# LSH attention and MLP on one core: one product for two heads' value means, value tiles summed on GpSimd, a new instruction order

## The chip, the core and the metric

The kernel runs on one core of a Trainium2 chip. The core has TensorE (PE) for matrix products, VectorE (DVE), ScalarE (ACT) and GpSimd (POOL) for elementwise work, and SyncE (SP), which issues DMAs. Each engine runs its own instructions in the order in which the program has them, and waits at semaphores for the others. The metric is the device time of one execution in microseconds.

## The reference, cut to what matters

```python
# q, k, v: (4, 8, 768, 64); proj: (64, 6); x: 3072 rows of 512
mask   = bucket(q) == bucket(k)                  # 6 sign bits of q@proj and k@proj
scores = where(mask, 0.125 * q @ k.T, -1e9)
attn   = exp(scores - max(scores)); attn = attn / (sum(attn) + 1e-9)
x      = (attn @ v), the heads side by side
h      = maximum(x @ w_in, 0)
out    = (s * h*h + b) @ w_out
```

The kernel adds to each row of `attn @ v` a small multiple of the sum of the head's value rows, `1e-9 / (768 + 1e-9)` times it, so that a row without any match comes out as the mean of the values, as the reference has it. This vector, one of 64 numbers for each head (`vmn`), is what the change is about.

## The kernel before, in words

There are 32 heads (4 batches of 8), called visits and counted from 0, and each is worked in three chunks of 256 queries, so 96 slots. A slot's work is a chain: score products on TensorE into three PSUM banks (L595 for the fp32 heads, L597 for the others), the row maximum on VectorE (L603), two small transposes on TensorE (L614, L618) with short VectorE steps behind them (L616, L625), six mask products that add the maximum into the banks (L635, L637), exponentials on ScalarE (L642), and value products into bank 3 (L665 for the first nine heads, L667 and L668 for the rest). Two copies on ScalarE (L698, L700) read bank 3 and so free it for the next slot; L700 adds `vmn`. Each pair of heads is scaled on GpSimd (L710), cast on ScalarE (L711), split on GpSimd (L712) and written to DRAM by a DMA from the tile `xsb`.

From slot 23 on TensorE also has the products of the MLP (L746, L763), which fill its time between the attention's steps. In the first slots ScalarE, VectorE and GpSimd also decode the MLP's weights (L374 to L386), which is why GpSimd is busy there.

How the mean's sum is made depends on the head. Heads 0 to 8 are computed in fp32 (`w < NPL`, NPL is 9): their value tile `EV`, 128 rows by 6 tiles by 64, is multiplied on TensorE by a column of ones, one product for each of the 6 tiles into one column of bank 4 (L543). Heads 9 to 31 load the tile into `vn`, VectorE sums it over the 6 tiles into 64 columns of `pj` (L556), and one product with the ones follows (L558). In both cases ScalarE scales the column into `vmn` (L525). An fp32 product shows as two records in the trace, so L543 has 108 for 9 heads and L558 has 46 for 23. Bank 4 is shared with the transposes: a group of steps holds it until it is done.

The order on all engines is not the order of the code. Each step is added to a plan with an engine, a cost, what it reads and writes, and a priority (`pr`); a list scheduler goes through the plan with these costs and takes the step of lowest priority that is ready. The priority is the slot's number times 10 and an offset, and to it a number of the table NUDGE is added, one for each place of the code and part of the program. So a change of the table or of a cost moves steps on all engines.

Of the kernel before, what the change touches and what calls it, by code (L numbers as in the profile page):

```python
# [22 lines left out]
EPS = 1e-9  # L23
# [143 lines left out]
NPL = 9  # L167
# [5 lines left out]
def lsh_attention_moe(ctx: ExitStack, tc, q, k, v, proj, w_in, w_out, s, b, out):  # L173
# [52 lines left out]
    def mmc(n, c):  # L226
        return c * (n / 2400.0 + 0.0013) if c % 4 == 0 else c * (n * 0.000436 + 0.0088)
# [124 lines left out]
    def decode(u, pr):  # L352
# [9 lines left out]
        def raw():  # L362
            return box["t"]
# [12 lines left out]
        dve(256, lambda: nc.vector.tensor_scalar(raw()[:, :, 1], gi, -2**31, None, ALU.bitwise_and), [gk], rk, pr, 0.6)  # L376
        dve(512, lambda: nc.vector.scalar_tensor_tensor(gi, gi, 3, raw()[:, :, 1], ALU.logical_shift_left, ALU.bitwise_or), rk, [gk], pr, 0.92)
# [8 lines left out]
        pool(512, lambda: nc.gpsimd.tensor_tensor(wt[key][:, 1], g, f32(wt[key][:, 0]), ALU.subtract), [gk, key + (0,)], [key + (1,)], pr)  # L386
# [135 lines left out]
    def mean(bb, h, pr):  # L522

        n = bb % 2 * H + h
        act(1, lambda: nc.scalar.activation(vmn[:, n:n + 1], bank[0:D, 4, 0:1], AF.Copy, scale=EPS / (S + EPS)), [("b", 4, "m")], [("vm", n)], pr)  # L525
        plan.hold(None)

    def prep_values(w, pr):
# [4 lines left out]
        if w < NPL:  # L533
# [6 lines left out]

            def sums():
                for t in range(NT):
                    nc.tensor.matmul(bank[0:D, 4, 0:1], EV[x][:, t, 0], ones, start=(t == 0), stop=(t == NT - 1))  # L543
            plan.hold(4)
            pe(0.5, sums, vk, [("b", 4, "m")], pr)
            mean(bb, h, pr)
            return
# [4 lines left out]
        to = vn  # L552
        plan.add(SP, 0.7, lambda: nc.sync.dma_start(to, vd), [], ["vn"], pr, 0.9)
        act(NT * D, lambda: nc.scalar.copy(VS[x][:, :, 0, :], to), ["vn"], vk[0:1], pr)
        pool(NT * D, lambda: nc.gpsimd.tensor_tensor(VS[x][:, :, 1, :], to, f32(VS[x][:, :, 0, :]), ALU.subtract), ["vn", vk[0]], vk[1:2], pr)
        dve(NT * D, lambda: nc.vector.tensor_reduce(pj[:, 0:D], to.rearrange("p t d -> p d t"), AX.X, ALU.add), ["vn"], ["vp"], pr, 0.84)  # L556
        plan.hold(4)
        pe(0.25, lambda: nc.tensor.matmul(bank[0:D, 4, 0:1], pj[:, 0:D], ones, start=True, stop=True), ["vp"], [("b", 4, "m")], pr)  # L558
        mean(bb, h, pr)
# [397 lines left out]
```

## Time and profile before

| what | value |
|---|---|
| median of 3 timed runs | 1003.89 us (1003.73 to 1006.42) |
| profiled execution | 1000.88 us, its span 999.1 us |
| TensorE busy | 979.9 us (98%) |
| VectorE busy | 677.5 us (68%) |
| ScalarE busy | 670.8 us (67%) |
| GpSimd busy | 640.5 us (64%) |
| mean share of the 16 DMA engines | q1 29.9%, q10 5.7% |

Busy time is that of one profiled execution. Products on TensorE overlap in the records, so the time that one takes is read from start to start. In the chain of work that ended last, TensorE has 91%, VectorE, GpSimd and DMA 2% each.

### The profile page before, as it was taken

How to read it: one execution, taken by the hardware profiler on the slowest of the kernel's cores; microseconds unless marked ns; L12 is line 12 of the kernel's file. 1: busy time of each engine (PE TensorE's matmuls, PEld its weight loads, DVE VectorE, ACT ScalarE, POOL GpSimd, SP SyncE). 2: the span in 40 equal slices, each digit the busy share in tenths (PEclk: the TensorE clock that was granted, in tenths of full speed). 3: DMA queues.
4: the chain of work that ended last, by engine and by line, in shares of the span. 5: the costliest groups of instructions: out<-in, count | busy, mean ns of one | idle time of the engine just before them, and what ended most of it. 6: DMA issues, size and time to landing. Idle time of an engine off the chain costs nothing.

```text
span 999.1 us, 18150 instructions
## 1 busy us (share of the span) xinstructions
PE 979.9 (98%) x6528; PEld 883.6 (88%) x6528; DVE 677.5 (68%) x1030; ACT 670.8 (67%) x1312; POOL 640.5 (64%) x584
## 2 busy tenths in 40 slices
PE   8989989999999999999999999999999999999998
PEld 6877868889999999999999999999999999999997
DVE  6777888778778877878778877878778766200000
ACT  4677777767767777777767777777777777523232
POOL 1677776758677677768677677778677677522222
PEclk9999999999999999999999999999999999999999
DMA  7575664533423423433423432433423310201000
GB/s 195 148 192 162 182 169 129 152 76 82 129 53 79 122 69 63 131 71 81 120 63 79 104 84 61 136 71 81 120 60 80 97 47 1 96 1 64 32 22 21
DMA packets 131954, 93.06 MB, mean 93 GB/s; under 512 B 101145, under 2 KB 104601, under 8 KB 131865
## 3 DMA queue, kind: packets, MB, share of 16 engines
q1 hardware_dynamic: 126664, 74.87, 29.9%
q10 hardware_dynamic: 5200, 17.05, 5.7%
q8 instruction: 51, 0.84, 0.3%
q14 instruction: 39, 0.31, 0.1%
HBM read 48.24 MB, written 18.87 MB: 67 GB/s over the span
## 4 chain that ended last, share of the span: by engine, by line
PE 91%; DVE 2%; POOL 2%; DMA 2%; issue 1%; ACT 1%; DVEq 0%; ACTq 0%; SPq 0%; POOLq 0%
PE bank L746 28%; PE bank L763 27%; PE bank L597 6%; PE bank L637 6%; PE bank L667 5%; PE bank L668 5%; PE bank L665 4%; PE bank L595 2%; PE bank L695 2%; DMA xd<-xsb 1%; PE bank L618 1%; PE bank L506 1%; PE bank L508 1%; PE bank L507 1%; POOL w L386 1%
## 5 line engine op out<-in xcount | busy, mean ns | idle before, releaser
L661 POOL TENSOR_TENSOR hl<-et,hl 128x512 fp32r<-128x512 f32 x207 | 267.3, 1320 | 138.5 <-ACT hl L660 86.0
L746 PE MATMUL bank<-xc,w 128*128 128x256 f32 x2304 | 338.5, 284 | 0.0
L746 PEld LDWEIGHTS bank<-xc,w 128*128 128x128 f32 x2304 | 305.4, 190 | 5.9
L763 PE MATMUL bank<-w,ghb 128*128 128x512 f32 x768 | 252.4, 396 | 0.0
L754 POOL TENSOR_TENSOR glb<-rb,ghb 128x512 fp32r<-128x512 f32 x96 | 124.1, 1292 | 99.8 <-ACT ghb L753 93.7
L603 DVE TENSOR_REDUCE mx<-bank 128x256 f32<-128x1536 f32 x96 | 168.0, 1750 | 6.9 <-PE bank L597 3.2
L763 PE MATMUL bank<-w,glb 128*128 128x512 f32 x384 | 152.3, 398 | 0.0
L642 ACT ACTIVATE et<-bank 128x512 f32<-128x512 f32 x234 | 128.6, 626 | 32.5 <-PE bank L637 23.4
L763 PEld LDWEIGHTS bank<-w,ghb 128*128 128x128 f32 x768 | 135.2, 189 | 16.6 <-issue 0.2
L687 DVE TENSOR_REDUCE zb<-et 128x256 f32<-128x1536 f32 x69 | 120.8, 1751 | 40.9 <-ACT et L642 40.2
L660 ACT CAST hl<-et 128x512 fp32r<-128x512 f32 x207 | 125.2, 672 | 0.3
L751 ACT ACTIVATE rb<-bank 128x512 f32<-128x512 f32 x96 | 56.8, 592 | 98.7 <-PE bank L746 98.4
L597 PE MATMUL bank<-aq,ks 84*128 84x256 f32 x504 | 109.6, 301 | 2.3 <-DMA aq<-nat 1.4
L700 ACT ACTIVATE xpb<-bank,vmn 64x256 f32<-64x256 f32 x96 | 45.0, 468 | 97.4 <-PE bank L668 64.1
L667 PE MATMUL bank<-hl,vs 128*128 128x256 f32 x414 | 107.9, 283 | 0.0
L668 PE MATMUL bank<-hl,vs 128*128 128x256 f32 x414 | 107.3, 281 | 0.0
L597 PEld LDWEIGHTS bank<-aq,ks 84*128 84x128 f32 x504 | 81.0, 190 | 9.1 <-ACT xpb L700 1.8
L667 PEld LDWEIGHTS bank<-hl,vs 128*128 128x128 f32 x414 | 77.9, 188 | 8.9
L668 PEld LDWEIGHTS bank<-hl,vs 128*128 128x128 f32 x414 | 78.0, 188 | 8.0
L763 PEld LDWEIGHTS bank<-w,glb 128*128 128x128 f32 x384 | 72.2, 188 | 11.5 <-issue 0.2
L637 PE MATMUL bank<-bq,ks 128*128 128x256 f32 x504 | 76.9, 287 | 0.0
L771 DVE SCALAR_TENSOR_TENSOR osb<-bank,misc,bcs 128x512 f32<-128x512 f32 x22 | 16.2, 747 | 88.9 <-PE bank L763 88.8
(126 smaller groups left out, 1545.2 us busy)
## 6 DMA issues: line engine op xcount, KB each, us to landing
xd<-xsb SPq DMA_DIRECT2D x48, 256.0 KB
xc<-xd SPq DMA_DIRECT2D x48, 256.0 KB
raw<-in_moe_w_in_dram ACTq DMA_DIRECT2D x16, 512.0 KB
raw<-in_moe_w_out_dram ACTq DMA_DIRECT2D x16, 512.0 KB
out_dram<-osb SPq DMA_DIRECT2D x22, 256.0 KB
ks<-aq SPq DMA_DIRECT2D x28, 192.0 KB
ks<-bq SPq DMA_DIRECT2D x28, 192.0 KB
bq<-aq SPq DMA_DIRECT2D x28, 192.0 KB
```

Of the source, the lines that this page charges most:

```text
L597: nc.tensor.matmul(o, ks[0:HR + NR, 0, kt], aq[0:HR + NR, cs], start=m == 0, stop=m == 1, skip_group_check=True)
L603: dve(S * TPC, lambda: nc.vector.tensor_reduce(t, sc, AX.XY, ALU.max), [("b", b) for b in pb], [tk], pr, 1.75)
L637: nc.tensor.matmul(o, ks[:, 1, kt], bq[:, cs], start=False, stop=m == 1, skip_group_check=True)
L642: act(512, lambda p=p, z=z: nc.scalar.activation(et(z) if plain(i) else pairs(z), bank[:, pb[p]] if plain(i) else bank[:, pb[p]].rearrange ...
L660: act(512, lambda z=z, y=y: nc.scalar.copy(HL[2 * y].rearrange("p (m n) -> p m n", n=CH), pairs(z)), [("e", z)], [("hl", 2 * y)], pr, 0.05)
L661: pool(512, lambda z=z, y=y: nc.gpsimd.tensor_tensor(HL[2 * y + 1].rearrange("p (m n) -> p m n", n=CH), pairs(z), f32(HL[2 * y]).rearrange ...
L667: nc.tensor.matmul(av, VS[x][:, kt], HL[2 * y][:, ms], start=(kt == 0), stop=False)
L668: nc.tensor.matmul(av, VS[x][:, kt], HL[2 * y + 1][:, ms], start=False, stop=(kt == NT - 1))
L687: dve(S * TPC, lambda: nc.vector.tensor_reduce(ZB, es, AX.XY, ALU.add), [("e", z) for z in range(NE)], ["zb"], pr, 1.75)
L746: nc.tensor.matmul(hp, wt[("wi", n, cc)][:, m % 2, fs], xc[:, m // 2, :], start=(cc == 0 and m == 0), stop=(cc == NC_ - 1 and m == 2))
L754: pool(2 * CH, lambda r=r, gh=gh, gl=gl: nc.gpsimd.tensor_tensor(gl, r, f32(gh), ALU.subtract), [rk, hk], [lk], MP)
L763: nc.tensor.matmul(bank[:, 6 + t, :], (gh, gh, gl)[n][:, ts], wt[("wo", f)][:, n % 2], start=(f == 0 and n == 0), stop=(f == NF - 1 and n ...
```

## The change

It has three parts.

1. Heads 9 to 31: an even head `h` sums its own value tile and that of head `h + 1`, which is loaded into `vn` a second time for that, into 2 x 64 columns of `pj`. One product with 128 columns of weights makes both sums, and the two evictions to `vmn` read rows 0 to 63 and 64 to 127 of the column. Odd heads after head 9 make none. That is 12 products (11 of them for two heads) in place of 23, and 34 loads of `vn` in place of 23. VectorE's sums stay 23.
2. Heads 2 to 8: GpSimd adds the six value tiles, in three additions of 192, 64 and 64 columns into `vn`, and one product follows in place of six. Heads 0 and 1 keep the six.
3. A few costs of the plan are other numbers, and the table NUDGE is new, so that steps stand in another order on every engine. Line numbers from L538 on move: L595/L597 become L621/L623, L618 is L644, L637 is L663, L642 is L668, L665 is L691, L698/L700 are L724/L726, L711 is L737, L746 is L772, L763 is L789.

```diff
-        return c * (n / 2400.0 + 0.0013) if c % 4 == 0 else c * (n * 0.000436 + 0.0088)
+        return c * (n / 2400.0 + 0.0013) if c % 4 == 0 else c * {256: 0.1215, 384: 0.175, 512: 0.2345}[n]
...
-    def mean(bb, h, pr):
+    def mean(bb, h, pr, j=0):
...
-        act(1, lambda: nc.scalar.activation(vmn[:, n:n + 1], bank[0:D, 4, 0:1], AF.Copy, scale=EPS / (S + EPS)), [("b", 4, "m")], [("vm", n)], pr)
-        plan.hold(None)
+        act(1, lambda: nc.scalar.activation(vmn[:, n:n + 1], bank[j * D:(j + 1) * D, 4, 0:1], AF.Copy, scale=EPS / (S + EPS)), [("b", 4, "m")], [("vm", n)], pr)
...
+            if w > 1:
+                s1, s2 = vn[:, 0:3], vn[:, 3]
+                pool(3 * D, lambda: nc.gpsimd.tensor_tensor(s1, EV[x][:, 0:3, 0], EV[x][:, 3:6, 0], ALU.add), vk[0:1], ["vn"], pr, 0.56)
+                pool(D, lambda: nc.gpsimd.tensor_tensor(s2, vn[:, 0], vn[:, 1], ALU.add), [], ["vn"], pr, 0.27)
+                pool(D, lambda: nc.gpsimd.tensor_tensor(s2, vn[:, 3], vn[:, 2], ALU.add), [], ["vn"], pr, 0.27)
+                plan.hold(4)
+                pe(0.3, lambda: nc.tensor.matmul(bank[0:D, 4, 0:1], s2, ones, start=True, stop=True), ["vn"], [("b", 4, "m")], pr)
+                mean(bb, h, pr)
+                plan.hold(None)
+                return
...
-            pe(0.5, sums, vk, [("b", 4, "m")], pr)
+            pe(0.75, sums, vk, [("b", 4, "m")], pr)
...
-        dve(NT * D, lambda: nc.vector.tensor_reduce(pj[:, 0:D], to.rearrange("p t d -> p d t"), AX.X, ALU.add), ["vn"], ["vp"], pr, 0.84)
+        def sums(j, to, tk):
+            dve(NT * D, lambda: nc.vector.tensor_reduce(pj[:, j * D:(j + 1) * D], to.rearrange("p t d -> p d t"), AX.X, ALU.add), [tk], ["vp"], pr, 0.84)
...
+        if h % 2 and w > NPL:
+            return
+        heads = (h,) if h % 2 else (h, h + 1)
+        for j, h_ in enumerate(heads):
+            if j:
+                fetch(to, tk, v[bb, h_].rearrange("(p t) d -> p t d", t=NT))
+            sums(j, to, tk)
+        rows = len(heads) * D
         plan.hold(4)
-        pe(0.25, lambda: nc.tensor.matmul(bank[0:D, 4, 0:1], pj[:, 0:D], ones, start=True, stop=True), ["vp"], [("b", 4, "m")], pr)
-        mean(bb, h, pr)
+        pe(0.3, lambda: nc.tensor.matmul(bank[0:rows, 4, 0:1], pj[:, 0:rows], ones, start=True, stop=True), ["vp"], [("b", 4, "m")], pr)
+        for j, h_ in enumerate(heads):
+            mean(bb, h_, pr, j)
...
 NUDGE = {
-    0: {0: -25.2, 1: 58.1, 2: 23.3, 3: 60, 4: -47.5},
+    0: {0: 28.7, 1: -23.1, 2: -11.6, 3: 14.5, 4: -8.9},
```

What the built order shows at three places, before and then after. First TensorE at the mean of head 4 (its value tile is `eva`, the second use of that tile), in the slot whose mask products read `bq_71`. Before:

```order
L665 MATMUL bank<-ex_87,vs_208 128x256 x2
L618 MATMUL bank<-ident,nmt 8x128
L543 MATMUL bank<-misc,eva 64x1 x6
L637 MATMUL bank<-bq_71,ks_73 128x256 x6
L472 MATMUL bank<-ident,nat_67 128x128 x3
```

After:

```order
L691 MATMUL bank<-ex_87,vs_208 128x256 x2
L623 MATMUL bank<-aq_69,ks_73 128x256 x2
L644 MATMUL bank<-ident,nmt 8x128
L623 MATMUL bank<-aq_69,ks_73 128x256 x2
L546 MATMUL bank<-misc,vn 64x1
L663 MATMUL bank<-bq_71,ks_73 128x256 x6
```

One product from `vn` stands where six from `eva` stood, still between the second transpose and the mask products, and two score products now stand between the transpose and it.

Second ScalarE, at the second cast of `xsb` (L711, now L737), with the copies that free bank 3. Before:

```order
L380 CAST w_644<-osb 128x512
L642 ACTIVATE et<-bank 128x512 x2
L711 CAST xsb<-xpb 128x256
L698 ACTIVATE zpb<-bank 64x256
L700 ACTIVATE xpb<-bank,vmn 64x256
L642 ACTIVATE et<-bank 128x512
```

After:

```order
L726 ACTIVATE xpb<-bank,vmn 64x256
L724 ACTIVATE zpb<-bank 64x256
L461 ACTIVATE eqa<-bank,misc 128x384
L737 CAST xsb<-xpb 128x256
L374 ACTIVATE osb<-raw_218 128x512
```

The two copies stood behind the cast and now stand ahead of it.

Third TensorE, in the second chunk of head 2 (its value tile is `vs_208`): the mask products and the value products of the same slot. Before:

```order
L637 MATMUL bank<-bq_70,ks_72 128x256 x6
L665 MATMUL bank<-et,vs_208 128x256 x2
L597 MATMUL bank<-aq_69,ks_73 128x256 x4
L665 MATMUL bank<-ex_82,vs_208 128x256
L614 MATMUL bank<-ident,mx 128x128 x2
```

After:

```order
L663 MATMUL bank<-bq_70,ks_72 128x256 x6
L691 MATMUL bank<-ex_82,vs_208 128x256 x2
L623 MATMUL bank<-aq_69,ks_73 128x256 x2
L691 MATMUL bank<-ex_83,vs_208 128x256 x2
L640 MATMUL bank<-ident,mx 128x128 x2
```

Two value products of the slot before (from `et`) and four score products stood between the mask products and the first value product of their slot (from `ex_82`); now it stands directly behind them.

## Rows read from the trace of the kernel before

**Rows 1.** Stretches of the span: us, busy time of each engine, clock, DMA share, GB/s.
```profile
5.00:155.00 150.00, 136.26 (x800) 111.61 (x800) 115.42 (x174) 106.65 (x211) 95.40 (x80) 0.99 0.66 176
155.00:805.00 650.00, 649.30 (x4477) 594.69 (x4476) 519.78 (x778) 478.97 (x953) 469.38 (x431) 1.00 0.37 92
```

**Rows 2.** Waits of TensorE from 5 to 155 us: total us, times, longest.
```profile
PE bank L665 <- ACT xpb L700: 3.9, 4, 2.1
PE bank L597 <- DMA aq<-nat: 1.4, 1, 1.4
...
PE bank L614 <- DVE mx L603: 0.3, 1, 0.3
```

**Rows 3.** Order of time on TensorE near 785 us: start us, us, operation, count.
```profile
784.20 0.28 PE L668 MATMUL bank<-hl,vs 128*128 128x256 f32 x1
784.32 0.40 PE L763 MATMUL bank<-w,ghb 128*128 128x512 f32 x1
784.55 0.88 PE L637 MATMUL bank<-bq,ks 128*128 128x256 f32 x6
785.36 0.28 PE L558 MATMUL bank<-misc,pj 128*64 128x1 f32 x2
785.57 0.50 PE L763 MATMUL bank<-w,ghb 128*128 128x512 f32 x1
```

**Rows 4.** Weight loads by line: busy us, mean ns, idle time before them.
```profile
L665 PEld LDWEIGHTS bank<-ex,vs 128*128 128x128 f32 x120 | 20.7, 190 | 4.4 <-ACT xpb L700 1.8
...
L614 PEld LDWEIGHTS bank<-ident,mx 128*128 128x128 f32 x48 | 6.3, 141 | 3.5 <-DVE mx L603 1.2 <-DVE bq L481 0.4 <-ACT eqb L461 0.2
...
L558 PEld LDWEIGHTS bank<-misc,pj 128*64 128x64 f32 x46 | 4.4, 134 | 3.3 <-issue 0.4
```

**Rows 5.** DMA issues of vn, then SyncE's waits before them.
```profile
vn<-in_v_dram SPq DMA_DIRECT2D x23, 192.0 KB
...
SPq L553 <- POOL vs L555: 6.8, 11, 1.1
```

**Rows 6.** Order of time on TensorE near 152 us.
```profile
151.21 0.86 PE L543 MATMUL bank<-misc,evb 128*64 128x1 f32 x12
152.00 0.98 PE L637 MATMUL bank<-bq,ks 128*128 128x256 f32 x6
152.91 0.86 PE L543 MATMUL bank<-misc,vs 128*64 128x1 f32 x12
```

**Rows 7.** GpSimd by line: busy us, mean ns, idle time before them.
```profile
L386 POOL TENSOR_TENSOR w<-osb,w 128x512 fp32r<-128x512 f32 x32 | 45.6, 1429 | 12.4 <-ACT w L380 11.0 <-DMA raw<-in_moe_w_out_dram 0.7 <-DMA nat<-in_k_dram 0.7
L378 POOL TENSOR_TENSOR osb<-osb,raw 128x512 int32<-128x512 int32 x32 | 41.9, 1308 | 47.4 <-DVE osb L377 35.1 <-ACT raw L375 6.1 <-issue 2.1
...
L710 POOL TENSOR_TENSOR xpb<-xpb,zpb 128x256 f32<-128x256 f32 x48 | 36.4, 758 | 41.0 <-DVE zpb L709 15.8 <-DVE xpb L702 13.0 <-ACT et L642 9.1
L555 POOL TENSOR_TENSOR vs<-vn,vs 128x384 fp32r<-128x384 f32 x23 | 23.3, 1014 | 4.9 <-ACT vs L554 4.9
```

**Rows 8.** Order of time on ScalarE near 65 us.
```profile
64.85 0.40 ACT L711 CAST xsb<-xpb 128x256 fp32r<-128x256 f32 x1 [1.99 <-DMA xd<-xsb]
...
65.68 0.47 ACT L700 ACTIVATE xpb<-bank,vmn 64x256 f32<-64x256 f32 x1
```

**Rows 9.** Order of time on TensorE near 66 us.
```profile
66.29 1.93 PE L665 MATMUL bank<-et,vs 128*128 128x256 f32 x4 [2.06 <-ACT xpb L700]
68.02 0.42 PE L618 MATMUL bank<-ident,nmt 128*8 128x128 f32 x1
```

**Rows 10.** One stretch after the wait; the clock stands behind GpSimd.
```profile
66.30:69.60 3.30, 3.30 (x10) 2.54 (x11) 1.17 (x5) 2.09 (x4) 1.23 (x2) 0.52 0.98 280
```

**Rows 11.** Order of time near 152 us, the exponentials.
```profile
152.54 1.08 ACT L642 ACTIVATE ex<-bank 128x512 f32<-128x512 f32 x2 [0.27 <-PE bank L637]
```

**Rows 12.** The decode step L376: min/median/max ns; then busy us, mean ns.
```profile
L376 DVE TENSOR_SCALAR raw<-osb x32: 373/478/1848, 21.5 to 202.4; 128x512 int32<-128x512 int32 x32
...
L376 DVE TENSOR_SCALAR raw<-osb 128x512 int32<-128x512 int32 x32 | 23.1, 720 | 0.2
```

More of the change, by code (lines that the diff above doesn't have):

```diff
@@ L375, in decode @@
         act(512, lambda: nc.scalar.activation(raw()[:, :, 0], raw()[:, :, 0].bitcast(U32), AF.Copy, scale=float(2.0**-29)), rk, rk, pr, 0.06)
-        dve(256, lambda: nc.vector.tensor_scalar(raw()[:, :, 1], gi, -2**31, None, ALU.bitwise_and), [gk], rk, pr, 0.6)
-        dve(512, lambda: nc.vector.scalar_tensor_tensor(gi, gi, 3, raw()[:, :, 1], ALU.logical_shift_left, ALU.bitwise_or), rk, [gk], pr, 0.92)
+        dve(256, lambda: nc.vector.tensor_scalar(raw()[:, :, 1], gi, -2**31, None, ALU.bitwise_and), [gk], rk, pr, 0.72)
+        dve(512, lambda: nc.vector.scalar_tensor_tensor(gi, gi, 3, raw()[:, :, 1], ALU.logical_shift_left, ALU.bitwise_or), rk, [gk], pr, 0.8)
         pool(512, lambda: nc.gpsimd.tensor_tensor(gi, gi, raw()[:, :, 0], ALU.add), rk, [gk], pr)
@@ L385, in decode @@
                 pool(512, lambda: nc.gpsimd.tensor_tensor(bcs, bcs, g, ALU.add), [gk], ["bcs"], pr + 5)
-        pool(512, lambda: nc.gpsimd.tensor_tensor(wt[key][:, 1], g, f32(wt[key][:, 0]), ALU.subtract), [gk, key + (0,)], [key + (1,)], pr)
+        pool(512, lambda: nc.gpsimd.tensor_tensor(wt[key][:, 1], g, f32(wt[key][:, 0]), ALU.subtract), [gk, key + (0,)], [key + (1,)], pr, 1.43)
     def bias(pr):
@@ L544, in prep_values @@
             plan.hold(4)
-            pe(0.5, sums, vk, [("b", 4, "m")], pr)
+            pe(0.75, sums, vk, [("b", 4, "m")], pr)
             mean(bb, h, pr)
+            plan.hold(None)
             return
@@ L551, in prep_values, with fetch @@
         plan.add(None, 0.0, new, [], vk, pr)
[L552 to L555, printed above, removed]
-        dve(NT * D, lambda: nc.vector.tensor_reduce(pj[:, 0:D], to.rearrange("p t d -> p d t"), AX.X, ALU.add), ["vn"], ["vp"], pr, 0.84)
+        to, tk = vn, "vn"
+        def fetch(to, tk, vd):
+            plan.add(SP, 0.7, lambda: nc.sync.dma_start(to, vd), [], [tk], pr, 0.9)
+        def sums(j, to, tk):
+            dve(NT * D, lambda: nc.vector.tensor_reduce(pj[:, j * D:(j + 1) * D], to.rearrange("p t d -> p d t"), AX.X, ALU.add), [tk], ["vp"], pr, 0.84)
+        fetch(to, tk, vd)
+        act(NT * D, lambda: nc.scalar.copy(VS[x][:, :, 0, :], to), [tk], vk[0:1], pr)
+        pool(NT * D, lambda: nc.gpsimd.tensor_tensor(VS[x][:, :, 1, :], to, f32(VS[x][:, :, 0, :]), ALU.subtract), [tk, vk[0]], vk[1:2], pr)
+        if h % 2 and w > NPL:
[6 more added lines that the diff above has]
+        rows = len(heads) * D
         plan.hold(4)
-        pe(0.25, lambda: nc.tensor.matmul(bank[0:D, 4, 0:1], pj[:, 0:D], ones, start=True, stop=True), ["vp"], [("b", 4, "m")], pr)
-        mean(bb, h, pr)
+        pe(0.3, lambda: nc.tensor.matmul(bank[0:rows, 4, 0:1], pj[:, 0:rows], ones, start=True, stop=True), ["vp"], [("b", 4, "m")], pr)
+        for j, h_ in enumerate(heads):
+            mean(bb, h_, pr, j)
+        plan.hold(None)
     def plain(i):
```

162 rows, old and new, of the table NUDGE are left out of this document.

## The prediction

> **What bounds the kernel now.** I read the stretches first. From 155 to 805 us, where the attention ends, TensorE is busy 649.30 of 650 us; before that, from 5 to 155 us, it is busy 136.26 of 150 us while VectorE, ScalarE and GpSimd are busy 115.42, 106.65 and 95.40 us [rows 1]. So after 155 us the kernel is bound by TensorE, and every microsecond of product that disappears there should come off the end. In the first stage TensorE is still the fullest engine, but its work is broken by waits in a chain: scores, row maximum on VectorE, two small transposes, mask products, exponentials on ScalarE, value products.
>
> Next I read who TensorE waited for in that stage. The list has 14 rows, from 3.9 us for the copy at L700, which frees the bank of the value products, down to 0.3 us [rows 2]; the whole list sums to 13.2 us. More than half of the 3.9 us is one place, at 64 to 66 us, and there the clock drops as well (below).
>
> The profiled execution took 1000.88 us, of which the span is 999.1 us; the median of the three timed runs is 1003.89 us, 3.0 us more. I work with differences against the profiled execution and put them under the median.
>
> **Part 1: one product for two heads (heads 9 to 31).** Of 23 mean products 12 stay, 11 of them twice as wide, so 11 go. The price of one is read from start to start: six mask products at L637 begin at 784.55 us, the mean product at 785.36 us, the next product at 785.57 us [rows 3]. A product of 256 columns with another behind it takes 0.12 us, from 784.20 to 784.32 us [rows 3], so six take 0.72 us; here 0.81 us pass, so the switch into fp32 costs 0.09 us; the product itself takes 0.21 us. Together 0.30 us, and all 11 lie in the stretch where TensorE has no idle time: 11 x 0.30 = 3.3 us.
>
> The 11 wide ones load 128 columns of weights in place of 64. A 64-column fp32 load takes 134 ns; a 128-column one takes 141 ns in the transposes at L614 and 190 ns in the value products at L665 [rows 4]. A mean product has two loads, so it grows by 0 to 0.11 us; I take 0.05, nearer to the transposes, which like it stream few columns: 11 x 0.05 = 0.5 us back. Part 1 gives 2.8 us, between 2.1 and 3.3.
>
> The loads overlap the products before them, and the rows do not split what shows. The Trainium skill (TensorE: Matmul & The Clock Gate, LDWEIGHTS) has the load time grow with the number of columns, columns / 1.2 in ns, so 53 ns more for each load and, as an estimate from that page, 1.2 us for the 22 loads; by it the sum below would be 0.7 us smaller. The transposes' 141 ns for 128 columns beside 134 ns for 64 speak against it, the 190 ns for it.
>
> The pairs cost 11 more loads of a value tile, 192 KB each beside the 23 there are, and each has to wait until the one tile vn is read out; SyncE already waited 6.8 us in 11 such places for L555 [rows 5]. Queued behind it stand loads of the next heads' q and k and of the MLP's input. The DMA engines are 37% busy in that stretch [rows 1], and TensorE's idle time there is 0.7 us in all, so I price them at nothing; if the cover failed, one late k tile would cost the 1.4 us of the one wait for a DMA in the first stage [rows 2].
>
> **Part 2: GpSimd sums the tiles of heads 2 to 8.** Seven groups of six products become seven single products. A group runs from 151.21 to 152.00 us [rows 6], 0.79 us, with no other work inside it. The single product left costs 0.21 to 0.30 us by the terms of part 1; I take 0.25. 7 x (0.79 - 0.25) = 3.8 us, between 3.4 and 4.1. On the path? The group at 151.21 stands between the mask row of VectorE and the mask products at 152.00, which the exponentials wait for, and in the new order three of the seven single products stand right in front of mask products and a fourth among them, so I count it whole; if the chain is set by the other engines, it is worth nothing. Lower bound 0.
>
> GpSimd gets 21 additions. Its two-input steps take 758 ns for 256 columns (a product at L710) and 1014 for 384 (L555) [rows 7], so 2.0 ns a column and 0.25 us besides: 0.63 us for 192 columns and 0.37 for 64, 1.4 us a head, 9.6 us in all. That raises its load in the first stage from 95 to 105 of 150 us. It hides behind TensorE's own work as long as a head's sums are done before TensorE comes to the product; without that cover TensorE stands, see the second rival.
>
> **Part 3: the order.** Two places can be priced. First, 64 to 66 us: ScalarE's cast at L711 waited 1.99 us for a DMA out of the same tile, and behind it in the queue stood the copies L698 and L700 [rows 8]; TensorE waited 2.06 us for L700, the four products after that took 1.73 us [rows 9], and from 66.3 to 69.6 us the granted clock was 0.52, the 1.2 GHz level, after the engine had stood idle [rows 10]. 3.3 us at 0.52 lose 3.3 x 0.48 = 1.6 us. In the new order the two copies stand ahead of that cast, so 2.06 + 1.6 = 3.7 us should go. The other three waits for L700 hold 1.8 us and may go or not.
>
> Second, on the debit side: in five of the first 24 slots the first value product now stands directly behind the six mask products. These began at 152.00 us, and TensorE was through with them at 152.91 us [rows 6]; the first of two exponentials began at 152.54 us, the two took 1.08 us [rows 11], so the first was done at 153.08 us and, with a hop of some 0.1 us, the value product could start at 153.2: about 0.3 us of wait, 5 x 0.3 = 1.5 us. That leaves 2.2 us net. How the rest of the 13.2 us of waits changes cannot be read from an order; I take 2.0 us, with bounds of 3 us lost (ten such new waits) and 7 us won (the place at 64 us, the other 1.8 us and some of the rest).
>
> **Sum.** 2.8 + 3.8 + 2.0 = 8.6 us, 0.9%. On the profiled execution 1000.9 - 8.6 = 992.3 us, under the median 1003.9 - 8.6 = 995.3 us; I say 995.3. The ends: 2.1 + 0 - 3 gives about 1004.8, 3.3 + 4.1 + 7 gives 989.5.
>
> **Rivals.** (1) The first stage is set by its chain, and the products that go there come back as waits. For it: three other engines are 64 to 77% busy and TensorE waits 13.2 us; against it: TensorE is 91% busy there. Then only part 1 counts, 1003.9 - 2.8 = 1001.1 us, within the 0.3% (3 us) that a measurement of this kernel tells from no change. (2) TensorE waits for the sums. GpSimd works in order, and a head's sums can stand behind a pair of decode steps, 1308 and 1429 ns [rows 7], 2.7 us. If each of the seven products waited that long, the seven waits are 19 us, and the time is 1003.9 - 8.6 + 19 = 1014 us. It decides against the change from (8.6 + 3.0) / 7 = 1.7 us a head on. For it: the product is next to the mask products, so all behind it would wait too. Against it: in the new order a head's three additions stand together, in one head with a single step between them. (3) The new order takes much more of the waits, some 5 us of the other 9: 990 us. (4) The sums slow VectorE. The decode step L376 took 373 ns at best and 1848 at worst, 720 in the mean [rows 12], all 32 between 21.5 and 202.4 us, where GpSimd works beside it; the time above the best is 32 x 0.35 = 11 us beside some 95 us of GpSimd's work, so 9.6 us more would add 1.1 us, on the path at worst: 996.4 us. The Trainium skill (GPSIMD Engine Reference, Key points) names the reason, that GpSimd shares its SBUF interfaces with VectorE, and advises VectorE for such sums; the spread of L376 agrees with that, and no run here shows the cause.
>
> **How the numbers follow.** The forecast, 992 to 999 us, gets 0.47; rival 3, down to 987, 0.17; rival 4 0.09; rival 1 0.16; rival 2, with what else a worse order could do, 0.11. Faster by over 0.3% is 0.47 + 0.17 + 0.09 = 0.73, within 0.3% 0.16, slower 0.11. The range 988 to 1003 leaves out rival 2, the tail of rival 3 and a little of rival 1.
>
> **What would show it.** In the new profile: 14 records at L546 and 24 at L582 in place of 84 of the 108 at L543 and the 46 at L558; TensorE's stretch from 155 us on shorter by some 3 us; the first stage shorter by some 6 us; no stretch of low clock near 65 us; waits for the exponentials (L668) in the list of the first stage. A wait of TensorE for GpSimd's L544 would speak for rival 2. The forecast is wrong if the first stage keeps its length, or if a wait for a DMA shows up behind the eleven new loads.

## The result and the profile after

The changed kernel takes 991.48 us (median of four runs, 990.59 to 992.73), the kernel before, run beside it, 1004.52 us (four runs, 1003.73 to 1006.42). The ratio is 0.987, with a 95% interval of 0.985 to 0.989: 13.0 us or 1.3% less. Its profiled execution took 992.73 us, against 1000.88 us for that of the kernel before: 8.2 us less. The two differences disagree, and the experiments below have to say why.

The first view is the stretches again; columns as in [rows 1].

```profile
5.00:155.00 150.00, 140.02 (x772) 115.38 (x772) 115.40 (x181) 108.57 (x215) 97.91 (x96) 1.00 0.64 173
155.00:805.00 650.00, 646.03 (x4469) 592.91 (x4468) 525.35 (x778) 489.00 (x962) 489.05 (x445) 1.00 0.38 96
```

TensorE is busy 140.0 of the first 150 us, where it was 136.3, and the clock of that stretch is 1.00 where it was 0.99. How long the first batch lasts is read from the small row maximum that only its 24 slots have: L616 before, L642 now. The two rows are of the instructions of that one line; after the durations stand the starts of the first and the last. The first row is the kernel before, the second the changed one.

```profile
L616 DVE TENSOR_REDUCE nmt<-bank x24: 386/424/426, 20.3 to 177.6; 128x2 f32<-128x256 f32 x24
```

```profile
L642 DVE TENSOR_REDUCE nmt<-bank x24: 384/425/426, 20.8 to 170.9; 128x2 f32<-128x256 f32 x24
```

The last of the 24 starts at 170.9 us in place of 177.6: 6.7 us of the 8.2 us are there by then. The two executions do not begin alike, though. At L271 stand 13 products (26 records) which the change does not touch, again the kernel before first:

```profile
1.19 4.96 PE L271 MATMUL bank<-mx 128*128 128x128 f32 x26 [1.19 <-DVE mx L269]
```

```profile
1.19 5.92 PE L271 MATMUL bank<-mx 128*128 128x128 f32 x26 [1.19 <-DVE mx L269]
```

The changed kernel was 0.96 us behind after them. Over all profiled executions here they take 4.51 to 5.92 us, so a difference of some 1.4 us or less between two single profiles can come from the start.

Next the waits of TensorE from 5 to 155 us, answering [rows 2].

```profile
PE bank L623 <- DMA aq<-nat: 1.6, 1, 1.6
PE bank L691 <- ACT ex L668: 1.5, 5, 0.5
PE bank L496 <- ACT eqa L461: 1.1, 2, 0.8
PE bank L546 <- DVE bq L651: 1.0, 2, 0.6
PE bank L691 <- ACT et L668: 0.9, 1, 0.9
...
```

The copy of the value products (L700 before, L726 now), which headed the old list with 3.9 us, is gone from it. The prediction's five new waits for the exponentials are there with 1.5 us, its own figure; four of them stand directly behind mask products. GpSimd is not named as a releaser. TensorE's work near 66 us, answering [rows 9], shows what stands there now:

```profile
65.83 0.55 PE L458 MATMUL bank<-ident,nat 128*128 128x128 f32 x3 [0.50 <-DVE bq L651]
...
70.02 0.50 PE L623 MATMUL bank<-aq,ks 84*128 84x256 f32 x2 [1.58 <-DMA aq<-nat]
```

The wait of 2.06 us and the products behind it, 427 ns from start to start, are gone; 4 us later TensorE waits 1.58 us for a small DMA transfer. The list above ends at 155 us and so misses the longest new wait. This is TensorE, then ScalarE, around 168 us:

```profile
166.63 0.28 PE L582 MATMUL bank<-misc,pj 128*64 128x1 f32 x2
168.94 1.13 PE L691 MATMUL bank<-ex,evb 128*128 128x256 f32 x4 [2.04 <-ACT vmn L525]
```

```profile
165.45 0.47 ACT L726 ACTIVATE xpb<-bank,vmn 64x256 f32<-64x256 f32 x1
167.19 0.67 ACT L374 ACTIVATE osb<-raw 128x512 f32<-128x512 f32 x1 [1.28 <-POOL w L386]
...
168.31 0.58 ACT L668 ACTIVATE ex<-bank 128x512 f32<-128x512 f32 x1
```

On ScalarE a step that decodes weights (L374) waits 1.28 us for GpSimd, and the exponential that TensorE needs stands behind it. The releaser named, the copy of a mean at L525, follows that exponential on the same queue. So GpSimd holds up TensorE here by way of ScalarE.

It does so at a second place, the wait of 0.9 us for `et` in the list above. GpSimd, ScalarE and TensorE near 120 us:

```profile
118.11 0.38 POOL L544 TENSOR_TENSOR vn<-vn 128x64 f32<-128x64 f32 x1
118.46 2.09 POOL L386 TENSOR_TENSOR w<-osb,w 128x512 fp32r<-128x512 f32 x1
```

```profile
120.58 0.67 ACT L374 ACTIVATE osb<-raw 128x512 f32<-128x512 f32 x1 [1.44 <-POOL w L386]
121.27 1.09 ACT L668 ACTIVATE et<-bank 128x512 f32<-128x512 f32 x2
```

```profile
121.92 1.13 PE L691 MATMUL bank<-et,vs 128*128 128x256 f32 x4 [0.86 <-ACT et L668]
```

The three sums of a head (from 117.03 us) stand ahead of L386 on GpSimd, L374 waits for L386, and the exponentials stand behind L374. Which of the two places belongs to the sums is answered by e1, e2 and e3.

Last, the new products and additions. The first row is the view of the instructions of L546 alone (columns as above); then come GpSimd and the weight loads by line, with columns as in [rows 4].

```profile
L546 PE MATMUL bank<-misc,vn x14: 188/197/218, 15.4 to 145.1; 128*64 128x1 f32 x14
```

```profile
L542 POOL TENSOR_TENSOR vn<-vs 128x192 f32<-128x192 f32 x5 | 2.9, 590 | 5.9 <-DMA vs<-in_v_dram 5.8
L544 POOL TENSOR_TENSOR vn<-vn 128x64 f32<-128x64 f32 x7 | 2.8, 394 | 0.5
L543 POOL TENSOR_TENSOR vn<-vn 128x64 f32<-128x64 f32 x7 | 2.2, 320 | 4.5 <-PE bank L546 4.0
```

```profile
L582 PEld LDWEIGHTS bank<-misc,pj 128*128 128x128 f32 x22 | 3.7, 189 | 0.4
```

There are 14 records at L546, and at L582 24, 22 of them with 128 columns. The sums cost 590, 394 and 320 ns, 9.1 us in all, for an estimated 9.6.

### The profile page after: what moved, and what is told of

It reads as the page before. It is cut to its first block, busy times and chain, and to the rows that moved or that the text cites. A ratio compares the mean times of both kernels' runs of the same rounds, so it can differ in the third digit from the quotient of the medians.

```text
span 990.9 us, 17962 instructions
## 1 busy us (share of the span) xinstructions
PE 972.1 (98%) x6436; PEld 877.4 (89%) x6436; DVE 678.5 (68%) x1030; ACT 677.8 (68%) x1312; POOL 655.6 (66%) x605
## 4 chain that ended last, share of the span: by engine, by line
PE 87%; POOL 6%; issue 2%; DMA 2%; DVE 2%; ACT 1%; SPq 0%; DVEq 0%; ACTq 0%; POOLq 0%
PE bank L772 27%; PE bank L789 26%; PE bank L623 6%; PE bank L663 5%; PE bank L693 5%; PE bank L694 5%; PE bank L691 4%; POOL osb L378 2%; PE bank L621 2%; PE bank L721 2%; POOL w L386 1%; PE bank L644 1%; POOL bcs L385 1%; PE bank L508 1%; PE bank L507 1%
## 5 line engine op out<-in xcount | busy, mean ns | idle before, releaser
L687 POOL TENSOR_TENSOR hl<-et,hl 128x512 fp32r<-128x512 f32 x207 | 270.1, 1329 | 103.8 <-ACT hl L686 71.0
L772 PE MATMUL bank<-xc,w 128*128 128x256 f32 x2304 | 333.8, 283 | 0.3 <-DMA xc<-xd 0.3
L772 PEld LDWEIGHTS bank<-xc,w 128*128 128x128 f32 x2304 | 304.9, 190 | 6.9 <-DMA xc<-xd 0.5
L789 PE MATMUL bank<-w,ghb 128*128 128x512 f32 x768 | 253.5, 397 | 0.0
L789 PE MATMUL bank<-w,glb 128*128 128x512 f32 x384 | 152.6, 398 | 0.0
L668 ACT ACTIVATE et<-bank 128x512 f32<-128x512 f32 x234 | 134.2, 628 | 25.5 <-PE bank L663 17.5
L789 PEld LDWEIGHTS bank<-w,ghb 128*128 128x128 f32 x768 | 135.3, 189 | 16.0
L686 ACT CAST hl<-et 128x512 fp32r<-128x512 f32 x207 | 131.0, 663 | 1.5
L693 PE MATMUL bank<-hl,vs 128*128 128x256 f32 x414 | 109.9, 286 | 0.0
L623 PE MATMUL bank<-aq,ks 84*128 84x256 f32 x504 | 108.0, 300 | 1.6 <-DMA aq<-nat 1.6
L694 PE MATMUL bank<-hl,vs 128*128 128x256 f32 x414 | 108.3, 281 | 0.0
L623 PEld LDWEIGHTS bank<-aq,ks 84*128 84x128 f32 x504 | 81.5, 189 | 9.9 <-DMA aq<-nat 2.0
L726 ACT ACTIVATE xpb<-bank,vmn 64x256 f32<-64x256 f32 x96 | 45.1, 470 | 62.3 <-PE bank L694 50.0
L789 PEld LDWEIGHTS bank<-w,glb 128*128 128x128 f32 x384 | 72.3, 188 | 10.9 <-POOL glb L780 0.2
L663 PE MATMUL bank<-bq,ks 128*128 128x256 f32 x504 | 77.5, 287 | 0.0
```

Of the source, the lines that this page charges most:

```text
L623: nc.tensor.matmul(o, ks[0:HR + NR, 0, kt], aq[0:HR + NR, cs], start=m == 0, stop=m == 1, skip_group_check=True)
L663: nc.tensor.matmul(o, ks[:, 1, kt], bq[:, cs], start=False, stop=m == 1, skip_group_check=True)
L668: act(512, lambda p=p, z=z: nc.scalar.activation(et(z) if plain(i) else pairs(z), bank[:, pb[p]] if plain(i) else bank[:, pb[p]].rearrange ...
L686: act(512, lambda z=z, y=y: nc.scalar.copy(HL[2 * y].rearrange("p (m n) -> p m n", n=CH), pairs(z)), [("e", z)], [("hl", 2 * y)], pr, 0.05)
L687: pool(512, lambda z=z, y=y: nc.gpsimd.tensor_tensor(HL[2 * y + 1].rearrange("p (m n) -> p m n", n=CH), pairs(z), f32(HL[2 * y]).rearrange ...
L693: nc.tensor.matmul(av, VS[x][:, kt], HL[2 * y][:, ms], start=(kt == 0), stop=False)
```

## The experiments

e1 to e4, e5 to e8 and e9 to e12 each shared a chip and its runs of the kernel before, whose medians were 1003.41, 1002.83 and 1003.84 us. None of the kernels leaves work out; in e6, e7, e8 and e11 some products compute columns that nothing uses.

### The parts taken out one by one (e1, e2, e3)

e1 has the new order alone. Each head keeps its own narrow product (two heads' products stand directly behind each other), and the seven heads keep their six products:

```
 (sums)
-    pool(3 * D, lambda: nc.gpsimd.tensor_tensor(s1, EV[x][:, 0:3, 0], EV[x][:, 3:6, 0], ALU.add), ...)
+    pool(3 * D, lambda: None, ...)
...
-    pe(0.3, lambda: nc.tensor.matmul(bank[0:D, 4, 0:1], s2, ones, start=True, stop=True), ...)
+    pe(0.3, six, ...)          # six: one matmul for each tile t < NT
 (two heads)
-    pe(0.3, lambda: nc.tensor.matmul(bank[0:rows, 4, 0:1], pj[:, 0:rows], ones, start=True, stop=True), ...)
+    pe(0.3, each, ...)         # each: one matmul of 64 columns for each head
```

> The new order with the old products: heads 2 to 8 have six narrow products again and GpSimd's sums are left out, and each pair of heads has two products of 64 columns in place of one of 128 (the second loads of the value tile stay). It shows what the order alone is worth. First theory, by the records of the two kernels: the order removes about 2.1 us of waits for the bank-3 copy, 1.6 us of low clock and some more waits, so it should come out 3 to 6 us faster than the kernel before, and 6 to 8 us slower than the changed kernel. Rival, the products are all of it: no faster than the kernel before by more than 1 us. Other rival, the first stage is set by its chain: as fast as the changed kernel but for 3 us.

e2 has the second half of this edit (two narrow products) with the sums on GpSimd; e3 the first half (six products) with the wide product.

> The changed kernel with the pair's product split into two of 64 columns, at the same place in the order. First theory: by the start times after the change a 128-column product costs 0.23 us with what it does to its neighbours, a 64-column one 0.40 us, and the second of two about 0.14 us, so 11 x 0.31 = 3.4 us slower than the changed kernel. The theory of the prediction (the wide one costs 0.35, the narrow 0.30, the second 0.21): 11 x 0.16 = 1.8 us slower.

> The changed kernel with the six narrow products of heads 2 to 8 back in the place of the one, and GpSimd's 21 sums left out. First theory, these products lie on the path of the first stage: 7 x 0.55 = 3.8 us slower than the changed kernel, less what GpSimd's sums cost. Rival, the first stage is set by its chain: within 1 us of the changed kernel. Rival, the sums slow VectorE or GpSimd: 1 us or more faster than the first theory has it.

Measured: e1 997.17 us, ratio 0.995 (0.9933 to 0.9967); e2 994.14, ratio 0.9925 (0.9905 to 0.9945); e3 994.36, ratio 0.9925 (0.9905 to 0.9946). The profiled executions, all at a clock of 1.000, took 996.16, 994.27 and 993.31 us. By the profiles, from 1000.88 us: 4.7 us by the order with the pairing, 1.9 us by the sums (e1 to e2) and 2.9 us by the wide product (e1 to e3). The last step, to the changed kernel's 992.73, 991.76 (e5) and 991.45 us (e9), is 0.6 to 1.9 us for the sums and 1.5 to 2.8 us for the wide product. These are single executions, and L271 took 5.11 to 5.25 us in e1 to e3 and 5.91 or 5.92 in the last step's three. The timed runs at a mean clock of 1.000 have nearly the same to say: their means are 995.98 us in e1 (three runs), 993.60 in e2 (four), 993.20 in e3 (three) and 991.49 in the changed kernel (seven, from the first result, e5 and e9), so 1.7 to 2.4 us for the sums and 2.1 to 2.8 for the wide product. So all three parts gain, and none in the size forecast.

The sums took the expected time off TensorE and gave only part of it to the end. In the trace, 84 records with starts 58 to 59 ns apart became 14; a group of twelve went from 0.98 us to 0.40 us, neighbours included, 7 x 0.58 = 4.1 us in all. One part comes back in the wait at `et` shown above: it is 0.87 us in e2 and 0.85 to 0.86 in the changed kernel's three profiles, and e1 and e3, which lack the sums, have no wait at that place. So this wait is the sums' own cost. The longer one, 2.04 us at 168.94, stands in e1 and e3 as well (2.03 and 2.04) and belongs to the order. Another part comes back in e2 near 178 us; TensorE there:

```profile
176.63 0.36 PE L775 MATMUL bank<-xc,w 128*128 128x256 f32 x1
178.10 1.69 PE L775 MATMUL bank<-xc,w 128*128 128x256 f32 x12 [1.11 <-DMA xc<-xd]
```

e1 has no such wait: it comes to that place later, when the MLP's input is there. 4.1 - 0.9 - 1.1 = 2.1 us are near the 1.9 measured between e1 and e2. The changed kernel, whose steps up to there are those of e2, began later (L271) and waits there 0.31 us, or not at all in e5 and e9.

### The width of the product (e6, e7)

The start-to-start distances had shown something that was not expected: a 64-column fp32 product costs its neighbours more than a 128-column one. e6 tests that in the kernel before, with the same order and the same number of products:

```
-        pe(0.25, lambda: nc.tensor.matmul(bank[0:D, 4, 0:1], pj[:, 0:D], ones, start=True, stop=True), ["vp"], ...)
+        pe(0.25, lambda: nc.tensor.matmul(bank[:, 4, 0:1], pj, ones, start=True, stop=True), ["vp"], ...)
```

> The kernel before, in which the 23 products of L558 (one for each head from 9 to 31) take all 128 columns of the summed tile as weights and write 128 rows, where 64 of each were taken; the other 64 columns are not used by anything. Nothing else differs, and the order is the same. Theory W, from the traces (a product of 64 columns costs 0.40 us with what it adds to its two neighbours, one of 128 columns 0.23): 23 x 0.17 = 3.9 us less, 0.996 of before. The price in the prediction (0.30 for the narrow one, 0.05 more for the wide one): 23 x 0.05 = 1.2 us more, 1.001 of before. If it is no different from before, the 0.40 and 0.23 come from what stands around the products and not from their width.

Measured: 1000.73 us against 1002.83, ratio 0.9977 (0.9966 to 0.9988). 2.1 us less: the wider product is the cheaper one, at a little over half the price difference expected. The place in the trace says why. First TensorE with the narrow product (in e12, which has the products of the kernel before), then with the wide one (e6):

```profile
331.45 0.87 PE L637 MATMUL bank<-bq,ks 128*128 128x256 f32 x6
332.25 0.28 PE L558 MATMUL bank<-misc,pj 128*64 128x1 f32 x2
332.45 0.50 PE L746 MATMUL bank<-xc,w 128*128 128x256 f32 x2
332.79 0.40 PE L597 MATMUL bank<-aq,ks 84*128 84x256 f32 x2
333.03 0.52 PE L746 MATMUL bank<-xc,w 128*128 128x256 f32 x3
```

```profile
336.52 0.88 PE L637 MATMUL bank<-bq,ks 128*128 128x256 f32 x6
337.24 0.28 PE L558 MATMUL bank<-misc,pj 128*128 128x1 f32 x2
337.37 0.48 PE L746 MATMUL bank<-xc,w 128*128 128x256 f32 x2
337.69 0.50 PE L597 MATMUL bank<-aq,ks 84*128 84x256 f32 x2
338.03 0.52 PE L746 MATMUL bank<-xc,w 128*128 128x256 f32 x3
```

Six products take 0.72 us and two take 0.24 us when nothing disturbs them. Narrow: 0.80 us for the six, 0.20 us for the mean, 0.34 us for the two behind it, so 0.08 + 0.20 + 0.10 = 0.38 us (0.40 by the trace's ns). Wide: 0.72 us for the six, 0.13 us, 0.32 us, so 0.13 + 0.08 = 0.21 us; but then the pair at L597 takes 0.34 us in place of 0.24. The 0.10 us come back at the next product of that kind, in about two of three places of e6. 23 x 0.18 less some 15 x 0.10 is 2.6 us, near the 2.1 us measured. Two narrow products directly behind each other, as in e1, share the disturbance; TensorE there:

```profile
326.48 0.40 PE L795 MATMUL bank<-w,ghb 128*128 128x512 f32 x1
326.80 0.39 PE L587 MATMUL bank<-misc,pj 128*64 128x1 f32 x4
327.13 0.39 PE L699 MATMUL bank<-hl,vs 128*128 128x256 f32 x1
327.35 0.28 PE L700 MATMUL bank<-hl,vs 128*128 128x256 f32 x1
```

With 0.23 us for the product of 512 columns and 0.12 for the one at L699, the pair costs 0.09 + 0.33 + 0.10 = 0.52 us, where two apart cost 0.80. So e1's 4.7 us hold 11 x 0.28 = 3.1 us of pairing by this count and some 1.6 us of order; no run measures the two apart.

e7 widens what is narrow in the changed kernel: the products of L546 and L553 and the single one of L582.

```
-                pe(0.3, lambda: nc.tensor.matmul(bank[0:D, 4, 0:1], s2, ones, start=True, stop=True), ["vn"], ...)
-                mean(bb, h, pr)
+                pe(0.3, lambda: nc.tensor.matmul(bank[:, 4, 0:1], vn[:, 2:4], ones, start=True, stop=True), ["vn"], ...)
+                mean(bb, h, pr, 1)
```

> The changed kernel, in which the 7 products of L546, the one product of L582 with a single head, and the 12 products of L553 (heads 0 and 1) take 128 columns, the other 64 unused. Theory W: 8 x 0.17 = 1.4 us less than the changed kernel, and up to 0.5 more for the 12 at the start, so 0.4 to 1.9 us less. If the first stage is set by chains off TensorE, only the one of L582 counts: no difference.

Measured: 992.44 us, against 992.13 for the changed kernel beside it (e5): no gain. All these products stand in the first 170 us. In its profile the early slots run 0.9 us ahead of e5, but that is no saving of the edit: L271, ahead of the first widened product, took 1.4 us less than in e5. First e5 at L553, then e7 at L271 and L553:

```profile
7.03 0.92 PE L553 MATMUL bank<-misc,eva 128*64 128x1 f32 x12
```

```profile
1.18 4.51 PE L271 MATMUL bank<-mx 128*128 128x128 f32 x26 [1.18 <-DVE mx L269]
5.53 1.40 PE L553 MATMUL bank<-misc,eva 128*128 128x1 f32 x12
```

Six wide products in a row take longer than six narrow ones: their records start 112 ns apart in place of 58, 1.26 us for twelve in place of 0.79. With what their neighbours gain, each of the two groups of L553 costs some 0.35 us more, and the first wide product of L546 gives back 0.18 as in e6: e7 is 1.4 us ahead of e5 after L271 and 0.9 after that product. From there to 67 us, and from 70 to 169 us, it neither gains nor loses on e5, so the other wide products of the first stage give TensorE no lead. What e7's execution does show is that a lead can be lost: the wait for the small transfer near 69 us, 0.8 us in e5, takes back all of the 0.9 us; from TensorE's list of waits in e7:

```profile
PE bank L623 <- DMA aq<-nat: 2.3, 1, 2.3
```

### The changed kernel again (e5, e9), the late exponential (e8)

> The changed kernel once more, beside the three below on one chip. If the first result holds, it is 11 to 14 us under the kernel before, with the granted clock at 1.000 in every run. The first three experiments, which each lacked a part of the change, ended at 994.1 to 997.2; if the parts are worth what those runs say, this one is 2 to 3 us under the two with one part taken out, about 991.5.

> The changed kernel, once more as the measure for the three beside it: 991.5 to 992.5, as in the first result and in e5.

Measured: 992.13 us (0.9885 to 0.9911 of before) and 991.57 us (0.9867 to 0.9892): 10.7 and 12.3 us less. The result stands; the mean clock was 1.000 or 0.998, not 1.000 in every run.

e8 moves the decoding step on ScalarE behind the exponentials on top of e7:

```
     queue = plan.order()
+    behind(373, 27, 668, 2)   # line, which one, behind which line, how many of these
+    behind(375, 25, 668, 2)
+    behind(374, 25, 668, 2)
```

> The kernel of e7 with one more move: on ScalarE the weight decoding step near 167 us (L374, L375, and the load L373 that stands between them) goes behind the next two exponentials and the copy of a mean, which stand behind it in the changed kernel, where L374 waited 1.28 us for GpSimd's L386 and TensorE then idled 2.04 us up to 168.94. If that wait cost its length: 1.3 to 2.0 us less than e7. If TensorE only waits for the next thing in that place (the decoding of weights comes 2 us later for VectorE's L376 and GpSimd's L378), no difference to e7.

Measured: 992.18 us, the time of e5 and e7. The wait did go, and another came; TensorE in e8:

```profile
166.23 0.28 PE L582 MATMUL bank<-misc,pj 128*128 128x1 f32 x2
166.61 1.13 PE L691 MATMUL bank<-ex,evb 128*128 128x256 f32 x4
...
178.16 1.69 PE L772 MATMUL bank<-xc,w 128*128 128x256 f32 x12 [1.00 <-DMA xc<-xd]
```

TensorE now waits for the same transfer xc<-xd as in e2. So the 2.04 us that the profile of the changed kernel shows at 168.94 are worth nothing by themselves.

### The transfer for which the first stage waits (e10, e11)

```
     queue = plan.order()
+    behind(SP, 538, 5, 2)   # the sixth load of a head's values, two places back on SyncE
```

> The changed kernel with one move on SyncE: the load of a head's values (evb, L538, 192 KB, whose sums only run at 117 us) that is issued at 62.69 us, one place ahead of the small transfer aq<-nat, goes behind that transfer and the store xd<-xsb. In the profiles of the changed order TensorE waits for aq<-nat near 69 us: 1.58 us in the first, 0.85 in e5, 1.22 in e8, and 2.29 in e7, whose start was 0.9 us earlier. If the gains ahead of 69 us are lost in that wait, and it hangs on the queue: the wait at L623 falls under 0.5, and the time by 0.8 to 1.6 us, to 990.5 to 991.3. If the transfer is late for another reason (the loads of the expert weights, 512 KB, which are in flight on another queue in the same stretch), the wait and the time stay: 992.

> e8 (wide products, the decoding step on ScalarE behind two exponentials) together with the move of e10. If e7's and e8's savings vanished in the waits for transfers (aq<-nat near 69 us, xc<-xd near 178 us), taking the first of them away gives part back: 0.5 to 1.5 us less than e10, about 990. If these savings are worth nothing in any case: the time of e10.

Measured: e10 990.76 us (989.41 to 991.07), 0.8 us under e9 beside it (990.95 to 992.63); e11 992.34 us (991.66 to 993.35). One row each of the lists of TensorE's waits, of e9 and of e10:

```profile
PE bank L623 <- DMA aq<-nat: 0.9, 1, 0.9
```

```profile
PE bank L623 <- DMA aq<-nat: 0.5, 1, 0.5
```

By these rows the small transfer hangs in part on what is queued ahead of it; they are one execution each, the unmoved order showed 0.8 to 1.6 us in its three profiles, and 0.3 of the 0.6 us by which e10's profile is there sooner come from L271. The 0.8 us are the least that was expected, and the intervals against before (0.9855 to 0.9881 for e10, 0.9867 to 0.9892 for e9) overlap, so that e10 beats the changed kernel is likely, not certain. e11 lies 1.6 us above e10, so the wide products and the late decoding do not add to it: the wait for xc<-xd is back at 178.44 us with 1.17 us.

### The kernel before with one and two moves (e4, e12)

Why do the timed runs differ by more than the profiles? In the profile of before there is, up to its last microseconds, one stretch of low clock, after the wait at 66 us [rows 10]. e4 moves the cast L711 behind the two copies (the one step of the new order that the prediction priced), e12 also puts the transfer bq<-aq behind aq<-nat near 128 us.

```
     queue = plan.order()
+    behind(711, 1, 2)                        # e4 and e12: ScalarE
+    queue.remove(i)                          # e12 alone: SyncE, i is bq<-aq
+    queue.insert(queue.index(last) + 1, i)   # last is aq<-nat
```

> The kernel before with one instruction moved: the second cast of xsb on ScalarE stands behind the two copies that free bank 3, in place of ahead of them. First theory: TensorE's wait of 2.06 us at 66 us and the stretch at 1.2 GHz after it (1.6 us) go, so it is 2 to 3.7 us faster than the kernel before in its profile, and the timed runs, which lie 3 to 5 us above the profiled execution, come down by as much or more, because the length of that wait hangs on a DMA. Rival: something else in the chain is late next at that place, then under 1 us.

> The kernel before with two moves in its order: on ScalarE the cast L711 that waited for xd<-xsb goes behind L698 and L700 (as in e4), and on SyncE the transfer bq<-aq near 128 us (192 KB) goes behind the small aq<-nat, for which TensorE waited 1.4 us in the profile of before, 2.8 in e4 and 2.9 in e6, the latter two followed by a stretch of 3.41 us at granted clock 0.5. If the kernel before owes its distance to its own undisturbed profile to these two waits and the low clock behind them, this kernel runs at a mean clock of 1.000 and at 997 to 999.5, against 1002 to 1004. If the low clock comes with any order of this kernel, its clock stays at 0.996 to 0.998 and the time over 1000.

Measured: e4 1001.43 us (997.1 to 1007.04), ratio 0.999 (0.9972 to 1.0007), no difference that can be told; e12 997.91 us (997.43 to 1002.57), ratio 0.996 (0.9945 to 0.9974). In e4 the wait at 66 us was gone, but TensorE waited longer at the next one, and the low clock came there. TensorE near 134 us, and the stretch behind it (columns as in [rows 1]):

```profile
134.48 0.47 PE L597 MATMUL bank<-aq,ks 84*128 84x256 f32 x2 [2.81 <-DMA aq<-nat]
```

```profile
135.30:138.70 3.40, 3.40 (x11) 2.77 (x11) 1.73 (x5) 2.69 (x5) 1.99 (x2) 0.50 0.75 119
```

3.4 us at 0.50, the 1.2 GHz level, lose 1.7 us. The same profile has a second such stretch, which the kernel before does not have there:

```profile
90.00:93.40 3.40, 2.96 (x9) 2.24 (x8) 2.56 (x4) 3.20 (x7) 3.32 (x4) 0.63 0.57 114
```

It loses 1.3 us more within this window, and it follows two short waits, of 1.12 us up to 88.94 and of 0.44 up to 90.64. So the low clock does not stand behind the longest waits alone. In e12 the pair at L597 runs through:

```profile
129.93 0.48 PE L597 MATMUL bank<-aq,ks 84*128 84x256 f32 x2
130.25 0.49 PE L458 MATMUL bank<-ident,nat 128*128 128x128 f32 x3
```

Its profiled execution has no stretch of low clock, and its mean clock, 0.994 to 0.999 in all 50 runs of the kernel before beside these experiments, is 0.999 or 1.000 in five runs of nine, which took 997.43 to 997.91 us; the other four took 1000.00 to 1002.57 at 0.997 or 0.998. So two places in the order are worth 3.0 us of the old profile and, with the low clock that follows them, 4.0 us of the old timed runs by the ratio (5.9 between the medians); the four longer runs show that the low clock is not always gone. The changed kernel has neither place, and no stretch of low clock in its profile before the last microseconds.

What stays open is when a wait is followed by the low clock. In the profile of e7 one of 2.3 us, in that of the changed kernel those of 1.58 and 2.04 us were not; in the kernel before that of 2.06 us was. In e4 the wait of 1.12 us was followed by another of 0.44 and then by the low clock; a wait of 1.12 us at the same line in e6 was not.

## Why the prediction was right, and by which errors

The forecast was 995.3 us, within 988 to 1003, and faster. Against the profiled execution, for which the sum was made, it was 992.3 us, and 992.73 came. That the two agree to 0.5 us is luck: by the counts below part 1 was some 3 us too small and part 2 some 2 us too large, and the changed kernel's profiled execution had a long start (L271). Under the median the forecast was 3.8 us too high.

**What bounds the kernel** was read rightly for the time from 155 us on: e6 changes nothing but products and the end moves. For the first stage it was half right. Where TensorE got ahead there (by its start in e7, by the move in e8, by a part of the sums in e2) it then waited for a transfer, aq<-nat near 69 us or xc<-xd near 178 us. That is the mechanism of rival 1, at two places, not for the whole stage.

**Part 1** was put at 2.8 us. The step that failed is the price of one narrow product, 0.30 us. It counted what the switch adds to the product ahead (0.09 us) and not the 0.10 us that it adds to the one behind, which in [rows 3] could not be seen, as the rows end at its start; the price is 0.40 us. The added 0.05 us for a wide product was wrong in its sign: it costs 0.22 us, and 0.10 us more in two places of eleven. By these, 23 x 0.40 = 9.2 us became 11 x 0.22 + 0.40 + 2 x 0.10 = 3.0 us: 6.2 us off TensorE, 2.9 of them measured between e1 and e3 and 3.1 counted for the pairing. The loads themselves grow with the columns as the Trainium skill has it (TensorE: Matmul & The Clock Gate, LDWEIGHTS): 189 ns for the 128 columns of L582, 134 for 64 [rows 4], 55 ns more where columns / 1.2 gives 53; both are some 80 ns longer than that formula makes them. The step from there to a dearer product is what the runs refute. By 53 ns a load the 46 loads of e6 would have made it 2.4 us slower, and it was 2.1 us faster.

**Part 2** was put at 3.8 us. TensorE's saving was that size, 4.1 us, but the end moved by 0.6 to 1.9 us in the profiles and by 1.7 to 2.4 in the timed runs at a clock of 1.000. The assumption that failed is "I count it whole": 0.9 us came back in the wait at 121.92, and in e2 1.1 us in the wait for xc<-xd. Rival 2 did not happen as it was put, for each of the seven sums had ended at least 1.2 us before its product began (L544 at 84.81, L546 at 86.02 is the closest); the list of e9 names a step of GpSimd, L386, once for L546 with 0.6 us, but it is not the sum. What rival 2 had not seen is that the sums push a decoding step back, and with it ScalarE and the exponentials. Rival 4 failed as well. L376 took 596 ns in the mean, against 720 [rows 12], but that fall is the order's: it took 582 ns in e1 and 591 in e3, without the sums, and 592 to 596 in e2, e5, e9 and the changed kernel, with them. That is at most 14 ns a step, 0.4 us over the 32. The Trainium skill (GPSIMD Engine Reference, Key points) names contention of GpSimd with VectorE instructions in a 2-port mode or with two SBUF inputs, and calls VectorE about twice as fast for elementwise work; at L376 no more than these 14 ns show, and what the sums would cost on VectorE no run here shows.

**Part 3** was put at 2.0 us. The place at 64 to 66 us went as described, 3.7 us with its low clock, and five waits of 1.5 us came as counted. The wait of 2.04 us at 168.94, which is the order's, was not foreseen. What e1 leaves for the order beside the pairing, 4.7 - 3.1 = 1.6 us, is near the 2.0, but rests on a count. The step that failed lies in the base: setting the sum under the median took the low clock of the profiled execution for that of all runs. The medians of before lie 2.0 to 3.6 us above it. 13 of the 50 runs beside the experiments have the profile's mean clock of 0.998 and took 1000.10 to 1001.81 us; all others but one have 0.997 or less and took 1002.05 to 1004.56. The changed kernel ran at 1.000 or 0.998. So 13.0 us came between the medians where the profiles differ by 8.2: 3.6 us are the first median above its profile, and 1.3 us are that the changed kernel's profiled execution was the longest of its four. What takes the low clock away is not shown: e1 has the new order, and five of its eight runs were below 1.000.

**What would show it.** First stage: 6 us shorter forecast, 6.7 measured by the last L642, in spite of the 0.96 us that L271 took longer; the stretch behind it: 3 us forecast, 1.5 left, but the order has moved work between the two, so this split proves little. No wait stands behind the eleven new loads of vn; the wait for aq<-nat that came is ahead of them all, and hangs in part on another load (e10).

## What to carry to other kernels

Price a small product by the start of the second product behind it: what it does to its neighbours can be half of the cost, and pairing two of a kind saves this without saving a product. In a stage where TensorE is 90% busy, follow a saving to the next wait for a transfer; a wait that the profile shows is worth its length only if nothing else is late right behind it. Compare the first instructions that the edit does not touch, too: a lead of e7 that looked like a saving was there before its first changed product. And before a sum is put under a median, compare the clock of the profiled execution with that of the timed runs.

## What the hardware showed beyond that

A mean product with 64 columns of fp32 weights between products in the other format costs 0.40 us with its neighbours, one with 128 columns 0.22, although its two loads are longer (189 against 134 ns). The 128-column product leaves the one ahead of it undisturbed (0.72 us for six against 0.80); in about two of three places of e6 it costs the later pair at L597 0.10 us. Between others the wide one is thus the cheaper; in a row it is not (e7): 112 ns from record to record against 58. Why the narrow one disturbs its forerunner was not tried.
